# Two key blocks per values matmul, a query with x stationary, and output products in two column tiles

## The chip, the cores and the metric

The kernel runs on one core of a Trainium2 chip. A core has a matrix engine (PE, with its weight loads shown apart as PEld), a vector engine (DVE), a scalar engine (ACT), a general engine (POOL), a sync engine (SP) that here issues nearly all loads, and sixteen DMA engines that move data between memory and the core's on-chip memory (SBUF). Matmul results go to PSUM, a second on-chip memory [...]. The metric is the time of one execution on the device in microseconds; the number compared is the median of several runs.

## The reference

A decode step for eight tokens mixes an attention branch and an MLP branch with a gate.

```python
def _A_ref(x, k_cache, v_cache, wq, wo):      # B=8, Sq=1, D=448, Hq=16, Hkv=8, Sk=4096, Dh=256
    W = min(4096, max(256, Sk // 4))          # 1024: only the last 1024 keys are used
    q = (x @ wq).reshape(B, Sq, Hq, Dh).transpose(0, 2, 1, 3)
    k = jnp.repeat(k_cache[:, :, Sk - W:, :], 2, axis=1)
    v = jnp.repeat(v_cache[:, :, Sk - W:, :], 2, axis=1)
    p = softmax(einsum("bhqd,bhkd->bhqk", q, k) * Dh ** -0.5)
    o = einsum("bhqk,bhkd->bhqd", p, v)
    return o.transpose(0, 2, 1, 3).reshape(B, Sq, Hq * Dh) @ wo
def _B_ref(x, w1, b1, w2, b2):                # F=1792
    y = layernorm(x)
    return gelu(y @ w1 + b1) @ w2 + b2
g = sigmoid((x * gate_w).sum(-1))
return g * _A_ref(x, ...) + (1 - g) * _B_ref(x, ...)
```

Everything is bf16 in memory. Keys and values of the window are 8 x 8 x 1024 x 256 elements each, 67 MB together; the four weight matrices add 10.6 MB.

## The kernel before

**Units.** The work on the cache is cut into 16 units (NQ), one for each token and each half of the eight key heads. A unit is four key heads (QUAD) with two query heads each, so eight query rows (RQ). Its keys are one load of 2 MB, its values another; in SBUF 32 partitions belong to one key head, and each partition holds 32 keys (NCK) of 256 elements.

**Loads.** `plan` is the list of all large loads in order: keys of unit 0, w1, the two parts of wq, w2, then keys of unit u and values of unit u-3 in turn, the last three values, and wo in six pieces. They pass through a ring of nine slots of 2 MB; `done()` marks slots as used up and lets `pump()` hand the next loads to SP's queue, where each waits for its slot. Instruction order on each engine is the order in which the Python code emits it (the schedule is manual).

**Per unit.** `transpose_keys` turns the keys with 64 PE transposes (L323) into PSUM and copies them out with ACT and DVE (L326, L328). `scores` multiplies them with the query rows, 16 matmuls of 512 columns in four column tiles of the PE array: each tile has its own 32 partitions of the result `S_ps`, and tiles run side by side. `top`, `expo`, `turn` and `bring` are the softmax of the unit before, placed between the transposes; `bring` leaves the turned weights in ET, 32 key blocks of eight columns, and `rsel`, which holds one over the row sum at the query rows' own places and zero elsewhere (`sel`). `values` (L416) streams the value rows of the 32 key blocks: 32 matmuls with an eight-column stationary block of ET and 256 columns of values, in turn into four column tiles of the PSUM tile PO, each accumulating eight blocks. DVE copies PO to `os_` (L430). `finish` multiplies `os_` with `rsel`, which picks for each query row the right row of `os_` and sums the four tiles, and writes the result into oT.

**Head.** Before the loop over units come `norm_and_gate`, the transposes of unit 0, `mlp_hidden` (the product with w1 and the activation), `query` (L333: 128 matmuls with a block of wq stationary and the eight tokens moving, result `qt` with the head dimension on partitions, eight scaled copies into qw), `scores` of unit 0 and `mlp_out` (L493: for each of 14 blocks of w2, and once for b2, four matmuls, one for each quarter of the 448 output columns, in four column tiles given by `quads`).

**Tail.** After the last unit's values and `finish`, `spread_rows` brings oT into a layout with all 128 partitions in use (oP), in two halves. `project` (L556) multiplies oP with wo: 32 steps j, each four matmuls of 112 columns in the four column tiles of `quads`, accumulating in A_ps. The order of issue is spread_rows of the first half, values and finish of the last unit, spread_rows of the second half, then the four calls of project; each waits for its piece of wo, of which the last comes in three parts. One DVE operation (L577) combines A_ps with the gate and the MLP output `mixb` into `res`, and four stores (L587), two issued by SP and two by ACT, write the four column quarters.

Of the kernel before, what the change touches and what calls it, by code (L numbers as in the profile page):

```python
# [8 lines left out]
ACT = mybir.ActivationFunctionType  # L9
ALU = mybir.AluOpType  # L10
AXIS = mybir.AxisListType
BF16 = mybir.dt.bfloat16
F32 = mybir.dt.float32
# [4 lines left out]
def kernel(  # L18
# [15 lines left out]
    nc = tc.nc  # L34
    P = nc.NUM_PARTITIONS

    NB, Sq, D = A_x.shape
    _, Hkv, Sk, Dh = A_k_cache.shape
    HD = A_wq.shape[1]
    Hq = HD // Dh  # L40
    rep = Hq // Hkv
    W = min(4096, max(256, Sk // 4))
# [3 lines left out]
    NJ = Dh // P  # L46
    NC = W // P
    NR = 3
# [2 lines left out]
    NF = F // P  # L51
    FH = F // 2
    HH = HD // 2
    QUAD = 4
    RQ = QUAD * rep
    NQ = NB * Hkv // QUAD
    SK = P // QUAD
    NCK = W // SK
# [10 lines left out]
    qscale = float(Dh) ** -0.5  # L69
# [118 lines left out]

    S_ps = ps_s.tile([P, W], F32)
    nc.vector.memset(S_ps[:], 0.0)  # L190
    PO = ps_po.tile([P, Dh], F32)
    nc.vector.memset(PO[:], 0.0)

    NX = NR + 2
    DQ = D // QUAD

    def quads(ps):
        return [
            (ps[32 * i : 32 * i + NB, :], slice(i * DQ, (i + 1) * DQ))
            for i in range(QUAD)  # L200
        ]

    xz = consts.tile([NB, 2, P], BF16)
# [3 lines left out]
    xT = consts.tile([P, NX, NB], BF16)  # L207
    yT = consts.tile([P, NX, NB], BF16)
    sel = consts.tile([P, RQ], F32)
    qw = consts.tile([P, NJ, NB, Hq // RQ, QUAD, RQ], BF16)  # L210
    oT = consts.tile([P, Hq, NJ, NB], BF16)
    gg = consts.tile([NB, 2], F32)
    spread = consts.tile([NB, QUAD, 32], F32)
    gg_s = consts.tile([P, 2], F32)
    ones_r = consts.tile([1, NB], BF16)
    mixb = consts.tile([P, DQ], F32)
    res = consts.tile([P, DQ], BF16)
    nc.vector.memset(spread[:], 0.0)
    nc.vector.memset(ones_r[:], 1.0)

# [8 lines left out]
    for h in range(2):  # L229
        nc.vector.tensor_copy(xz[:, h, h::2], x_sb[:, DM:D])  # L230
    transposed(xT, x_sb, xz)
    nc.vector.reduce_sum(
        sel[:], ident[:].rearrange("p (a s) -> p s a", a=QUAD)[:, 0:RQ, :], axis=AXIS.X
    )
    perm = consts.tile([P, P], BF16)
    nc.vector.tensor_copy(
# [5 lines left out]
    for a in range(QUAD):  # L242
# [3 lines left out]
            axis=AXIS.X,  # L246
# [6 lines left out]
    def norm_and_gate():  # L253
        stats = consts.tile([NB, nc.vector.BN_STATS_DIM], F32)
        nc.vector.bn_stats(stats[:], x_sb[:])
        mv = consts.tile([NB, nc.vector.BN_AGGR_DIM], F32)
        nc.vector.bn_aggr(mv[:], stats[:])
        eps_t = consts.tile([NB, 1], F32)
        nc.vector.memset(eps_t[:], 1e-5)
        rstd = consts.tile([NB, 1], F32)  # L260
        nc.scalar.activation(rstd[:], mv[:, 1:2], ACT.Sqrt, bias=eps_t[:], scale=1.0)
        nc.vector.reciprocal(rstd[:], rstd[:])
        y_sb = consts.tile([NB, D], BF16)
        nc.vector.tensor_scalar(
            y_sb[:],
            x_sb[:],
            scalar1=mv[:, 0:1],
            scalar2=rstd[:],
            op0=ALU.subtract,
            op1=ALU.mult,  # L270
        )
        for h in range(2):
            nc.vector.tensor_copy(yz[:, h, h::2], y_sb[:, DM:D])
        transposed(yT, y_sb, yz)
        prod = consts.tile([NB, D], F32)
        gl = consts.tile([NB, 1], F32)
        nc.vector.scalar_tensor_tensor(
            prod[:],
            in0=x_sb[:],
            scalar=1.0,  # L280
            in1=gw_b[:],
            op0=ALU.mult,
            op1=ALU.mult,
            accum_out=gl[:],
        )
        gth = consts.tile([NB, 1], F32)
        nc.scalar.activation(gth[:], gl[:], ACT.Tanh, scale=0.5)
        nc.vector.tensor_scalar(
            gg[:, 0:1], gth[:], 0.5, 0.5, op0=ALU.mult, op1=ALU.add
        )  # L290
        nc.vector.tensor_scalar(
            gg[:, 1:2], gth[:], -0.5, 0.5, op0=ALU.mult, op1=ALU.add
        )
        nc.vector.tensor_copy(
            spread[:, :, 0:NB],
            ident[0:NB, 0:NB]
            .rearrange("p (o b) -> p o b", o=1)
            .to_broadcast([NB, QUAD, NB]),
        )
        gp = ps_misc.tile([P, 2], F32, tag="misc", name="gp")  # L300
        nc.tensor.matmul(
            gp[:],
            lhsT=spread[:].rearrange("p i b -> p (i b)"),
            rhs=gg[:],
            start=True,
            stop=True,
        )
        nc.vector.tensor_copy(gg_s[:], gp[:])
# [22 lines left out]
        done()  # L331

    def query():  # L333
        qt = ps_misc.tile([P, Hq * NJ, NB], F32, tag="misc", name="qt")
        for r in range(NR + 1):
            w, o = slot("wq", r // 2), (r % 2) * HD
            for k in range(Hq * NJ):
                col = (k // NJ) * Dh + (k % NJ) * P
                half, c = divmod(col, HH) if r == NR else (0, col)
                nc.tensor.matmul(  # L340
                    qt[:, k, :],
                    lhsT=w[:, o + c : o + c + P],
                    rhs=xT[:, r + half, :],
                    start=(r == 0 and k == 0),
                    stop=(r == NR),
                    skip_group_check=True,
                )
        done(2)
        qv = qt[:].rearrange("p (g a i j) b -> p a j b g i", g=Hq // RQ, a=QUAD, i=rep)
        for a in range(QUAD):  # L350
            for j in range(NJ):
                nc.vector.tensor_scalar_mul(  # L352
                    qw[:, j, :, :, a, a * rep : (a + 1) * rep], qv[:, a, j], qscale
                )

    def scores(u):
# [37 lines left out]
    def bring(u):  # L394
        EB, selr = soft.pop(u)
        sm = ps_sm.tile([P, NCK + 1, RQ], F32, tag="sm", name="sm")
        nc.tensor.matmul(  # L397
            sm[:, 0:NCK, :], lhsT=perm[:], rhs=EB[:, :, 0:RQ], start=True, stop=True
        )
        nc.tensor.matmul(sm[:, NCK, :], lhsT=ones_f[:], rhs=selr[:], start=True, stop=True)  # L400
        ET = opool.tile([P, NCK, RQ], BF16, tag="ET", name="ET")
        nc.vector.tensor_copy(ET[:], sm[:, 0:NCK, :])  # L402
        rb = epool.tile([P, RQ], F32, tag="rb", name="rb")
        nc.vector.reciprocal(rb[:], sm[:, NCK, :])
        rsel = opool.tile([P, RQ], F32, tag="rsel", name="rsel")
        nc.vector.tensor_tensor(rsel[:], rb[:], sel[:], op=ALU.mult)
        soft[u] = (ET, rsel)

    def steps(u):
# [6 lines left out]
    def values(u):  # L416
        ET, rsel = soft.pop(u)
        vn = slot("v", u)
        for c in range(NCK):
            t = c % QUAD  # L420
            nc.tensor.matmul(  # L421
                PO[32 * t : 32 * t + RQ, :],
                lhsT=ET[:, c, 0:RQ],
                rhs=vn[:, c * Dh : (c + 1) * Dh],
                start=(c < QUAD),
                stop=(c >= NCK - QUAD),
            )
        done()
        os_ = epool.tile([P, Dh], F32, tag="os", name="os_")
        nc.vector.tensor_copy(os_[:], PO[:])  # L430
        soft[u] = (os_, rsel)

    def finish(u):
# [57 lines left out]
        return hs  # L491

    def mlp_out(hs):  # L493
        bb = ps_misc.tile([P, DQ], F32, tag="misc", name="bb")
        nc.vector.memset(bb[:], 0.0)
        for c in range(NF):
            w = slot("w2")
            for dst, cols in quads(bb):
                nc.tensor.matmul(
                    dst,  # L500
                    lhsT=hs[:, c, :],
                    rhs=w[:, c * D + cols.start : c * D + cols.stop],
                    start=(c == 0),
                    stop=False,
                )
        for dst, cols in quads(bb):
            nc.tensor.matmul(
                dst, lhsT=ones_r[:], rhs=b2_r[:, cols], start=False, stop=True
            )
        done()  # L510
        nc.vector.tensor_scalar_mul(mixb[:], bb[:], gg_s[:, 1:2])
# [20 lines left out]
    finish(u - 2)  # L532
    bring(u)
    values(u - 1)
    A_ps = ps_misc.tile([P, DQ], F32, tag="misc", name="A_ps")
    nc.vector.memset(A_ps[:], 0.0)
    finish(u - 1)
    oP = consts.tile([P, NJ8, NHQ, NB], BF16)
# [17 lines left out]
    def project(q):  # L556
        w = slot("wo", q - q % 2)
        for j in range(NJ8):
            o = ((q % 2) * NJ8 + j) * D
            for dst, cols in quads(A_ps):  # L560
                nc.tensor.matmul(  # L561
                    dst,
                    lhsT=oP[:, j, q, :],
                    rhs=w[:, o + cols.start : o + cols.stop],
                    start=(q == 0 and j == 0),
                    stop=(q == NHQ - 1 and j == NJ8 - 1),
                )
# [14 lines left out]
        op0=ALU.mult,  # L582
        op1=ALU.add,
    )
    for i, (src, cols) in enumerate(quads(res)):
        eng = nc.sync if i % 2 == 0 else nc.scalar
        eng.dma_start(out_f[:, cols], src)  # L587

# [29 lines left out]
```

## Time and profile before

| | us |
|---|---|
| median of 9 runs | 195.43 |
| lowest and highest | 195.28, 195.67 |
| the profiled execution | 195.28 |
| its span, first to last instruction | 193.5 |
| PE busy | 148.6 (77%) |
| PE weight loads busy | 110.7 (57%) |
| DVE busy | 112.4 (58%) |
| ACT busy | 82.9 (43%) |
| data moved | 78.02 MB, mean 403 GB/s |

The profile is of one execution. Its span is cut into 40 equal slices; in the rows of digits each digit is the busy share of a slice in tenths, and PEclk is the clock that the matrix engine was granted, in tenths of full speed. The queue rows give packets, megabytes and the time of the packets as a share of sixteen DMA engines over the span. Lines of the timeline give start, duration, engine, source line, operation, result and operands, count, and in brackets how long the engine had been idle before it and what ended the wait. Windows give the same measures for a stretch of time. The chain follows the work that ended last back to what released it.

### The profile page before, as it was taken

How to read it: one execution, taken by the hardware profiler on the slowest of the kernel's cores; microseconds unless marked ns; L12 is line 12 of the kernel's file. 1: busy time of each engine (PE TensorE's matmuls, PEld its weight loads, DVE VectorE, ACT ScalarE, POOL GpSimd, SP SyncE). 2: the span in 40 equal slices, each digit the busy share in tenths (PEclk: the TensorE clock that was granted, in tenths of full speed). 3: DMA queues.
4: the chain of work that ended last, by engine and by line, in shares of the span. 5: the costliest groups of instructions: out<-in, count | busy, mean ns of one | idle time of the engine just before them, and what ended most of it. 6: DMA issues, size and time to landing. Idle time of an engine off the chain costs nothing.

```text
span 193.5 us, 5200 instructions
## 1 busy us (share of the span) xinstructions
PE 148.6 (77%) x2334; PEld 110.7 (57%) x2334; DVE 112.4 (58%) x259; ACT 82.9 (43%) x101; POOL 0.8 (0%) x7
## 2 busy tenths in 40 slices
PE   1399968989999898987768787877878787946652
PEld 0399927675665767574637373737474646534441
DVE  7531342787866869684747575666666666653100
ACT  2352003675754828372708182827272727320000
POOL 1000000000000000000000000000000000000000
PEclk9997566999999999999999999999999999995555
DMA  4999999999999999999999999999999999999960
GB/s 176 428 423 415 432 424 428 417 430 423 430 423 430 420 423 423 427 425 423 423 430 423 430 417 425 423 427 427 427 430 423 427 417 430 420 423 422 407 248 7
DMA packets 6744, 78.02 MB, mean 403 GB/s; under 512 B 945, under 2 KB 1346, under 8 KB 1986
## 3 DMA queue, kind: packets, MB, share of 16 engines
q1 hardware_dynamic: 6512, 77.67, 95.3%
q8 instruction: 18, 0.29, 0.6%
q10 hardware_dynamic: 210, 0.02, 0.2%
q14 instruction: 4, 0.03, 0.0%
HBM read 77.68 MB, written 0.01 MB: 401 GB/s over the span
## 4 chain that ended last, share of the span: by engine, by line
DMA 86%; PE 7%; ACT 4%; ACTq 1%; issue 0%; DVE 0%; SPq 0%
DMA slot<-in_A_k_cache_dram 51%; DMA slot<-in_A_v_cache_dram 20%; DMA slot<-in_A_wo_dram 10%; DMA b_sb<-in_B_b_dram 4%; PE ktp L323 4%; ACT kt L326 3%; PE S_ps L361 2%; ACT E L381 1%; PE PO L421 1%; ACTq L174 0%; PE A_ps L561 0%; DVE res L577 0%; PE sm L400 0%; ACTq L181 0%; ACTq L178 0%
## 5 line engine op out<-in xcount | busy, mean ns | idle before, releaser
L326 ACT COPY kt<-ktp 128x1024 bf16<-128x1024 bf16 x64 | 63.2, 1017 | 74.4 <-PE ktp L323 74.4
L323 PE MATMUL ktp<-ident,slot 128*128 128x128 bf16 x1024 | 71.1, 226 | 22.3 <-ACT kt L326 10.8
L323 PEld LDWEIGHTS <-slot 128*128 128x128 bf16 x1024 | 65.0, 103 | 29.4 <-issue 16.1
L328 DVE COPY kt<-ktp 128x1024 bf16<-128x1024 bf16 x64 | 41.3, 684 | 16.4 <-PE ktp L323 16.4
L373 DVE TENSOR_REDUCE nmx<-S_ps 128x1 f32<-128x1024 f32 x16 | 19.6, 1225 | 22.6 <-PE S_ps L361 22.6
L361 PE MATMUL S_ps<-kt,qw 128*8 128x512 bf16 x256 | 32.3, 627 | 0.3 <-DVE qw L352 0.3
L389 DVE STREAM_TRANSPOSE EB<-E 128x1024 bf16<-128x1024 bf16 x16 | 19.9, 1245 | 7.2 <-ACT E L381 6.9
L421 PE MATMUL PO<-slot,ET 128*8 128x256 bf16 x512 | 18.4, 290 | 3.4 <-DMA slot<-in_A_v_cache_dram 3.4
L381 ACT ACTIVATE E<-S_ps,nmx 128x1024 bf16<-128x1024 f32 x16 | 17.9, 1120 | 3.3 <-DVE nmx L374 3.3
L421 PEld LDWEIGHTS <-ET 128*8 128x8 bf16 x512 | 11.9, 90 | 6.7 <-issue 3.5
L361 PEld LDWEIGHTS <-qw 128*8 128x8 bf16 x256 | 7.3, 95 | 12.0 <-issue 10.4
L402 DVE CAST ET<-sm 128x256 bf16<-128x256 f32 x16 | 6.6, 414 | 0.5 <-PE sm L400 0.5
L561 PE MATMUL A_ps<-slot,oP 128*8 128x112 bf16 x128 | 4.1, 291 | 2.4 <-DMA slot<-in_A_wo_dram 2.3
L400 PE MATMUL sm<-selr,ones_f 128*128 128x8 f32 x32 | 5.2, 233 | 0.0
L441 DVE CAST oT<-sm 128x16 bf16<-128x16 f32 x16 | 3.5, 219 | 2.8 <-PE sm L438 2.8
L400 PEld LDWEIGHTS sm<-selr,ones_f 128*128 128x128 f32 x32 | 4.8, 188 | 0.4 <-issue 0.4
L561 PEld LDWEIGHTS <-oP 128*8 128x8 bf16 x128 | 2.9, 114 | 3.4 <-issue 3.4
L397 PE MATMUL sm<-EB,perm 128*128 128x256 bf16 x16 | 4.4, 272 | 0.3 <-DVE oT L441 0.3
L340 PE MATMUL qt<-xT,slot 128*128 128x8 bf16 x128 | 3.6, 168 | 0.4 <-DVE z L471 0.4
L340 PEld LDWEIGHTS <-slot 128*128 128x128 bf16 x128 | 3.6, 104 | 0.4 <-issue 0.3
L577 DVE SCALAR_TENSOR_TENSOR res<-A_ps,gg_s,mixb 128x112 bf16<-128x112 f32 x1 | 0.3, 333 | 5.9 <-PE A_ps L561 5.9
L471 DVE TENSOR_TENSOR z<-hT,b_sb 128x112 f32<-128x112 f32 x1 | 0.3, 275 | 5.5 <-PE hT L461 5.5
(122 smaller groups left out, 75.5 us busy)
## 6 DMA issues: line engine op xcount, KB each, us to landing
slot<-in_A_v_cache_dram SPq DMA_DIRECT2D x16, 2048.0 KB, 38.8
slot<-in_A_k_cache_dram SPq DMA_DIRECT2D x15, 2048.0 KB, 36.0
slot<-in_A_wo_dram SPq DMA_DIRECT2D x3, 896.0 KB, 32.1
slot<-in_A_k_cache_dram SPq DMA_DIRECT2D x2, 1024.0 KB, 7.5
slot<-in_A_wq_dram SPq DMA_DIRECT2D x1, 2048.0 KB
slot<-in_B_w_dram SPq DMA_DIRECT2D x1, 1568.0 KB
slot<-in_B_w_dram SPq DMA_DIRECT2D x1, 1344.0 KB, 10.2
slot<-in_A_wq_dram SPq DMA_DIRECT2D x1, 1024.0 KB
```

The lines of the kernel that those rows point to most:

```text
L323: nc.tensor.transpose(ktp[:, c, :], kn[:, o : o + P], ident[:])
L326: nc.scalar.copy(dst, ktp[:])
L328: nc.vector.tensor_copy(dst, ktp[:])
L340: nc.tensor.matmul(qt[:, k, :], lhsT=w[:, o + c : o + c + P], rhs=xT[:, r + half, :], start=(r == 0 and k == 0), stop=(r == NR), skip_grou ...
L361: nc.tensor.matmul(S_ps[32 * a : 32 * a + RQ, hf * CH * SK : (hf + 1) * CH * SK], lhsT=qw[:, j, b, half, a, :], rhs=KT[hf][:, j, :, a::QUA ...
L373: nc.vector.reduce_max(nmx[:], S_ps[:], axis=AXIS.X, negate=True)
L381: nc.scalar.activation(E[:], S_ps[:], ACT.Exp, bias=nmx[:], scale=1.0, accum_out=rowsum[:])
L389: nc.vector.transpose(EB[:].rearrange("p c r -> p (c r)"), E[:])
L400: nc.tensor.matmul(sm[:, NCK, :], lhsT=ones_f[:], rhs=selr[:], start=True, stop=True)
L402: nc.vector.tensor_copy(ET[:], sm[:, 0:NCK, :])
L421: nc.tensor.matmul(PO[32 * t : 32 * t + RQ, :], lhsT=ET[:, c, 0:RQ], rhs=vn[:, c * Dh : (c + 1) * Dh], start=(c < QUAD), stop=(c >= NCK - ...
L561: nc.tensor.matmul(dst, lhsT=oP[:, j, q, :], rhs=w[:, o + cols.start : o + cols.stop], start=(q == 0 and j == 0), stop=(q == NHQ - 1 and j ...
```

## The change

There are four edits, and some constants and masks for them.

Values: the stationary operand is two key blocks of ET side by side (16 columns), the moving operand the two blocks' values side by side (512 columns). The product holds four parts, of which only the two with equal block are wanted: rows 0 to 7 of a tile with the first 256 columns, rows 8 to 15 with the second. [...] In place of the copy, one DVE operation multiplies the first half by a mask (`own`, column 0) and a second adds the second half times the other mask (column 1); `rsel` is built with `sel2`, which has a one at both places of a query row.

Query: x is stationary (eight columns) and wq moves in 512 columns, into four column tiles of S_ps, 32 matmuls; ACT copies the result with the scale to bf16, eight transposes of 128 x 128 bring the head dimension to partitions, and eight DVE copies write qw.

MLP output and projection: `halves` takes the place of `quads`: two column tiles, at partitions 0 and 64, of 224 columns each. The tiles bb, A_ps, mixb and res are twice as wide, and there are two stores of the output, one issued by SP and one by ACT.

```diff
-    PO = ps_po.tile([P, Dh], F32)
+    PO = ps_po.tile([P, PAIR, Dh], F32)          # PAIR = 2
...
-    def quads(ps):
+    def halves(ps):
         return [
-            (ps[32 * i : 32 * i + NB, :], slice(i * DQ, (i + 1) * DQ))
-            for i in range(QUAD)
+            (ps[64 * i : 64 * i + NB, :], slice(i * DO, (i + 1) * DO))   # DO = 224
+            for i in range(OT)                                           # OT = 2
         ]
...
+    halfs = ident[:].rearrange("p (a s) -> p s a", a=QUAD)
+    for i in range(PAIR):
+        nc.vector.reduce_sum(
+            own[:, i : i + 1], halfs[:, i * RQ : (i + 1) * RQ, :], axis=AXIS.XY
+        )
+    nc.vector.reduce_sum(
+        sel2[:],
+        ident[:]
+        .rearrange("p (a h s) -> p s a h", a=QUAD, s=RQ)[:, :, :, 0:PAIR],
+        axis=AXIS.XY,
+    )
...
     def query():
-        qt = ps_misc.tile([P, Hq * NJ, NB], F32, tag="misc", name="qt")
         for r in range(NR + 1):
             w, o = slot("wq", r // 2), (r % 2) * HD
-            for k in range(Hq * NJ):
-                col = (k // NJ) * Dh + (k % NJ) * P
-                half, c = divmod(col, HH) if r == NR else (0, col)
-                nc.tensor.matmul(
-                    qt[:, k, :],
-                    lhsT=w[:, o + c : o + c + P],
-                    rhs=xT[:, r + half, :],
...
+            for n in range(W // QN):                                     # QN = 512
+                for t in range(QUAD):
+                    col = t * W + n * QN
+                    half, c = divmod(col, HH) if r == NR else (0, col)
+                    nc.tensor.matmul(
+                        S_ps[32 * t : 32 * t + NB, n * QN : (n + 1) * QN],
+                        lhsT=xT[:, r + half, :],
+                        rhs=w[:, o + c : o + c + QN],
...
         done(2)
-        qv = qt[:].rearrange("p (g a i j) b -> p a j b g i", g=Hq // RQ, a=QUAD, i=rep)
+        qs = consts.tile([P, W], BF16)
+        nc.scalar.activation(qs[:], S_ps[:], ACT.Copy, scale=qscale)
+        qt = ps_kt.tile([P, NC, P], BF16, tag="ktp", name="qt")
+        for m in range(NC):
+            nc.tensor.transpose(qt[:, m, :], qs[:, m * P : (m + 1) * P], ident[:])
+        qv = qt[:].rearrange(
+            "p (c i j) (g d s) -> p d c j s g i", c=2, i=rep, j=NJ, g=Hq // RQ, d=2
+        )
         for a in range(QUAD):
             for j in range(NJ):
-                nc.vector.tensor_scalar_mul(
-                    qw[:, j, :, :, a, a * rep : (a + 1) * rep], qv[:, a, j], qscale
+                nc.vector.tensor_copy(
+                    qw[:, j, :, :, a, a * rep : (a + 1) * rep],
+                    qv[:, a // 2, a % 2, j, 0:NB],
                 )
...
-        nc.vector.tensor_tensor(rsel[:], rb[:], sel[:], op=ALU.mult)
+        nc.vector.tensor_tensor(rsel[:], rb[:], sel2[:], op=ALU.mult)
...
     def values(u):
-        for c in range(NCK):
+        NG = NCK // PAIR
+        for c in range(NG):
             t = c % QUAD
             nc.tensor.matmul(
-                PO[32 * t : 32 * t + RQ, :],
-                lhsT=ET[:, c, 0:RQ],
-                rhs=vn[:, c * Dh : (c + 1) * Dh],
+                PO[32 * t : 32 * t + PAIR * RQ],
+                lhsT=ET[:, PAIR * c : PAIR * (c + 1), :],
+                rhs=vn[:, PAIR * c * Dh : PAIR * (c + 1) * Dh],
...
-        nc.vector.tensor_copy(os_[:], PO[:])
+        nc.vector.tensor_scalar_mul(os_[:], PO[:, 0, :], own[:, 0:1])
+        nc.vector.scalar_tensor_tensor(
+            os_[:], in0=PO[:, 1, :], scalar=own[:, 1:2], in1=os_[:],
+            op0=ALU.mult, op1=ALU.add,
+        )
...
-            for dst, cols in quads(bb):
+            for dst, cols in halves(bb):        # and the same for b2, A_ps and res
```

## The prediction

> **What bounds the kernel now.** I read the slices first, then the chain that ended last, then the queues.
>
> ```profile
> PEclk9997566999999999999999999999999999995555
> DMA  4999999999999999999999999999999999999960
> DMA 86%; PE 7%; ACT 4%; ACTq 1%; issue 0%; DVE 0%; SPq 0%
> q1 hardware_dynamic: 6512, 77.67, 95.3%
> q8 instruction: 18, 0.29, 0.6%
> ```
>
> The DMA engines are full from the second slice to the next-to-last, and the chain is 86% transfers. So time is won in two ways only: the last transfer lands sooner, or less work follows it. PE's clock is halved in the last four slices, which matters for that work. The q8 row is the third thing to see: 18 packets that carry instructions, 0.6% of 16 engines' 193.5 us, so 18.6 us of engine time or 1.03 us each, 16 KB each.
>
> Next the end of the load stream in half-microsecond windows (the last two columns are the DMA share and GB/s):
>
> ```profile
> 184.50:185.00 0.50, 0.50 1.05 416
> 185.50:186.00 0.50, 0.50 0.60 233
> 187.50:188.00 0.50, 0.50 0.51 190
> 188.50:189.00 0.50, 0.50 0.07 25
> 189.00:189.50 0.50, 0.50 0.05 18
> ```
>
> The stream does not stop at once. From 185.3 about nine engines of sixteen still work (0.55 to 0.61), and from 188.2 only one (1/16 is 0.06). The trace's landing marks, one per engine and transfer, say the same: of the last wo piece the first mark is at 185.23, the fifteenth at 188.75, the sixteenth at 189.84. One engine ends 1.09 us after all others, and the kernel waits for it.
>
> Why is it late? I set the start of each q8 packet against the PE instructions started by then (a matmul and its weight load are two): the 9th at 91.0 us against 2254, the 17th at 180.9 against 4348, the 18th at 188.0 against 4588. That is one packet per 256 instructions. In the marks, at 80.25 the last engine is 0.04 us behind the fifteenth, but after the 9th packet one mark lies 1.08 us behind the other fifteen (100.95 against 99.87), after the 10th two do, after the 16th eight do; after the 17th one is alone again (185.35 against 184.25). I read this as eight engines taking the packets in turn, each losing about 1.08 us per packet; the one that gets the 1st, 9th and 17th decides the end.
>
> **The change part by part.** *PE's instruction count.* Values: 32 matmuls become 16 in each of 16 units, -256. Query: 128 become 32 and 8 transposes, -88. MLP output: 60 become 30, -30. Projection: 128 become 64, -64. Together -438 of 2334, leaving 1896, or 3792 PE instructions with the weight loads: 14 packets (3584) and not a 15th (3840). No engine then gets a third. In before, after 14 packets and until the 17th, the marks lay 3.54 us from first to last (151.82 to 155.36, 171.43 to 174.97); the first mark of the last piece, 185.23, belongs to an engine that takes no packets. New end: 185.23 + 3.52 to 3.54 = 188.75, **1.09 us sooner**. The other wo pieces move alike: 182.1, 184.25, 186.45, 187.6, 188.2.
>
> Here a rule speaks against the change. The Trainium skill, "Runtime: NRT & Kernel Launch", section Instruction fetch mechanics, says that fetches come in 16 KiB blocks of 256 instructions (the trace agrees) and that crossing a block costs "one DMA tail-bump, mostly hidden". By it this term is 0. It is hidden for PE, but the row has 1.03 us of one engine per packet, and here the slowest engine sets the end. I take the row. A bound on the other side: VectorE's own code grows by about 19 instructions, and a further fetch on q14 (8 KB, some 0.3 us each) may fall on the last engine: 0 to +0.3, I take 0.
>
> *The head.* Three reduces (L232's row has 0.20 for one) and a larger PO memset (+0.27) delay VectorE by 0.9. Query: 32 matmuls of 512 columns cost 3.4 to 5.1 at half clock (16 of the scores' took 2.55 at 25.08) against 3.55, then an activation over 1024 elements (L381: 1.12) and 8 transposes (0.6 to 0.9), then eight copies as before (0.9). mlp_out takes up to 1.7 more. In all 3 to 7 us later. What hides it:
>
> ```profile
> 51.45 0.54 SPq L109 DMA_DIRECT2D slot<-in_A_v_cache_dram  x1
> 52.44 0.54 SPq L109 DMA_DIRECT2D slot<-in_A_k_cache_dram  x1
> 60.94 0.54 SPq L109 DMA_DIRECT2D slot<-in_A_k_cache_dram  x1
> slot<-in_A_v_cache_dram SPq DMA_DIRECT2D x16, 2048.0 KB, 38.8
> ```
>
> The load issued at 51.45 lands at 80.25, 28.8 us later, when its own transfer is some 4.9: about 24 us of loads stand queued at the thinnest place, so slots given back 7 us late starve nothing. Beyond 24 us each further one would be paid in full. I price the head at 0.
>
> *The loop.* Values stream 16 x 512 columns instead of 32 x 256, in four tiles as before: no change. VectorE gets two masked operations for one copy. The copy is 0.425 (L430, 256 elements). L511 and L577, the same two forms on 112 elements, took 0.333; one element more costs 0.95 ns (L402's 256 took 414 ns, L552's 128 took 292), 144 more 0.14, so 0.47 each and 0.03 between: 0.97, **+0.55 per unit**. While it catches up, PE gives K slots back every 8.1 to 8.5 us (the lines above); with 0.55 that stays under the 9.8 us in which a unit's K and V land. Price 0, until a unit costs more than 9.8.
>
> *The tail.* Here nothing covers:
>
> ```profile
> 181.84 0.42 DVE L430 COPY os__3037<-PO 128x256 f32<-128x256 f32 x1 [2.36 <-PE PO L421]
> 185.39 0.92 PE L561 MATMUL A_ps<-slot,oP 128*8 128x112 bf16 x32 [0.62 <-DMA slot<-in_A_wo_dram]
> 187.57 0.92 PE L561 MATMUL A_ps<-slot,oP 128*8 128x112 bf16 x32 [1.27 <-DMA slot<-in_A_wo_dram]
> 189.88 0.36 PE L561 MATMUL A_ps<-slot,oP 128*8 128x112 bf16 x8 [0.22 <-DMA slot<-in_A_wo_dram]
> 190.29 0.33 DVE L577 SCALAR_TENSOR_TENSOR res<-A_ps,gg_s,mixb 128x112 bf16<-128x112 f32 x1 [5.91 <-PE A_ps L561]
> 190.65 0.70 SPq L587 DMA_DIRECT2D out_dram<-res  x2
> ```
>
> The last V lands at 179.88 in both kernels (the 17th packet comes after it). Behind the PO copy queue finish, spread_rows and project, so project starts at 183.78 + 0.55 = 184.33. One step j streams two tiles of 224 columns instead of four of 112. At the halved clock 256 columns took 0.213 (values at 179.92: 8 rounds in 1.88 less a 0.2 drain), so 224 take 0.187 and all 32 rounds **5.97 instead of 2.99**. In before projection waited for each wo piece; now the pieces come sooner and PE is behind them. Cold all the way it ends at 184.33 + 5.97 + 0.18 drain = 190.48, where before ended at 190.25. Warm soon enough, it ends 0.35 after the last landing: 188.79 + 0.35 = 189.14.
>
> Will it warm? "TensorE: Matmul & The Clock Gate" (Trainium skill, Part 1) says that the clock goes up after a busy window of about 3.4 us, free-running. The trace's clock steps lie on such a grid (17.16, 27.40, 30.82, 34.23, 174.18). In the window 23.99 to 27.40, 2.3 us of streaming (scores) were enough; in 174.18 to 177.59, 1.9 us (values) were not. By the row the clock rises at the first grid point after 184.33 + 2.2 = 186.5, somewhere up to 189.9 as the grid falls; its middle is 188.2. Half of what is then left remains: 188.2 + (190.30 - 188.2)/2 = 189.25, drain 0.17. By the rule's full window the middle is 189.5 and streaming ends at 189.9. I take the row, as it is this kernel's own streaming.
>
> Then res: 0.333 + 112 x 0.95 ns = 0.44 (+0.11). Output: each queue issues one transfer instead of two; the four landed at 191.87, 192.04, 192.25 and 192.47, and the first two remain: **-0.43**.
>
> *Sum.* Res ends at 189.42 + 0.04 + 0.44 = 189.90 against 190.62: -0.72; with the output -1.15. The profiled execution took 195.28 (span 193.5, 1.78 around it), so 194.13; the median of the runs, 195.43, is 0.15 above it, so **194.3**. By the clock rule's window it would be -0.50, 194.9; by the fetch rule (no sooner landing) about 195.1.
>
> **Rivals.** *Projection stays cold* (two tiles may not count as busy): res ends at 190.96, +0.34, with the output -0.09: 195.3. For: the clock never rose in the old tail. Against: there PE streamed under 2 us per window, here without a break. *The packets don't decide the end* (another order of engines, or a late q14 fetch): landing 189.84 as now, q3 streams behind it, res ends 0.1 to 0.6 later: 195.1 to 195.6. Against: marks and packets match one by one. *Two tiles don't overlap* (slower): each round costs two streams. Cold that would be 64 x 0.187 = 12.0 and end at 196.5; with the clock up from about 187.5 it ends near 192.0, so res at 192.6, +2.0, less 0.43: 197.0. It decides as soon as a cold round takes over 0.20. For: no pair of tiles 64 apart is in the trace. Against: four tiles do overlap (32 matmuls of 112 columns in 0.92).
>
> **How the numbers follow.** Likeliest case 0.70 (its own range, over the grid, 193.9 to 195.1), cold 0.17, packets don't decide 0.07, no overlap 0.06. The range takes in all but the last: 193.8 to 195.6. A difference of 0.2%, 0.39 us, is about what can be told here: faster 0.71 (nearly all of the first case, little of the third), same 0.22, slower 0.07.
>
> **What would show it.** q8 with 14 packets; no window with one engine alone; last wo landing near 188.75; project starting near 184.33 and streaming without gaps; clock back to full between 186.5 and 190; the res operation at 0.44; two output transfers. The prediction is wrong if the head empties the queue (a gap in the DMA slices), if a unit passes 9.8 us, or if the number of PE instructions is not 3792.

## The result, and the profile after

The changed kernel takes **194.53 us** in the median (194.04 to 194.82, ten runs), the kernel before 195.52 (195.28 to 195.79, 31 runs). The ratio is **0.9947, with a 95% interval of 0.9939 to 0.9955**: 0.99 us faster, where 1.15 was forecast. The execution that was profiled took 194.64 with a span of 192.9, so it shows only 0.6 of the gain in span. That difference is one of the things to explain.

The page of the changed kernel, first its span, the clock and DMA slices, the queues and the shares of the chain:

```profile
span 192.9 us, 4344 instructions
PEclk9999697999999999999999999999999999975559
DMA  5999999999999999999999999999999999999960
q1 hardware_dynamic: 6496, 77.67, 95.5%
q8 instruction: 15, 0.25, 0.5%
DMA 60%; PE 24%; ACT 7%; DVE 5%; issue 1%; ACTq 0%; SPq 0%; DVEq 0%
```

The loads fill the DMA slices as before. Instruction packets on q8 fell from 18 to 15, and the clock is back at full in the last slice. In before the chain that ended last came in through the last wo load (start, length, what):

```profile
170.13 19.71 DMA slot<-in_A_wo_dram
```

Now it comes in through the last values load, which landed at 179.89, and from there it runs over values, masked operations, finish and spread to projection without another load. Of the lines from there on, two:

```profile
179.93 1.91 PE PO L446 x13
184.68 4.75 PE A_ps L594 x63
```

So projection, not its data, is what ends last. The end of the load stream in half-microsecond windows (length, clock, DMA share, GB/s):

```profile
185.50:186.00 0.50, 0.50 0.62 244
187.50:188.00 0.50, 0.50 0.33 112
188.50:189.00 0.50, 1.00 0.00 0
189.00:189.50 0.50, 1.00 0.00 0
```

In before, the windows from 188.5 still showed one engine (0.07 and 0.05). Here they are empty. The landing marks of the last wo piece say it exactly: fourteenth 188.26, fifteenth 188.31, sixteenth 188.72; before they were 188.75 for the fifteenth and 189.84 for the sixteenth. The timeline of the tail (start, length, engine, operation):

```profile
181.86 0.48 DVE L455 TENSOR_SCALAR os__2685<-PO,own 128x256 f32<-128x256 f32 x1 [1.71 <-PE PO L446]
182.38 0.48 DVE L456 SCALAR_TENSOR_TENSOR os__2685<-PO,own,os__2685 128x256 f32<-128x256 f32 x1
184.50 4.92 PE L594 MATMUL A_ps<-slot,oP 128*8 128x224 bf16 x63
189.46 0.45 DVE L610 SCALAR_TENSOR_TENSOR res<-A_ps,gg_s,mixb 128x224 bf16<-128x224 f32 x1 [4.41 <-PE A_ps L594]
189.93 0.37 SPq L620 DMA_DIRECT2D out_dram<-res  x1
```

The two masked operations stand where one copy stood. Projection runs in one piece without waiting for wo, and `res` ends at 189.91 instead of 190.62. The last store lands at 191.35 instead of 192.47, 1.12 sooner. Yet the span is only 0.6 shorter: half a microsecond was lost behind the last store. It is in SP's instructions of the kernel's close, where SP waits for one pair of semaphores (the counters by which a transfer tells that it has landed) after the other (shortest, median and longest in ns, then first and last start), of the kernel before:

```profile
L613 SPq EVENT_SEMAPHORE  x7: 17/28/28, 192.3 to 193.4; - x7
```

and of the changed one:

```profile
L646 SPq EVENT_SEMAPHORE  x7: 17/28/1013, 190.4 to 192.8; - x7
```

In before, SP's instruction behind the last store's landing came 0.02 us after it (192.47, 192.49). In the changed kernel the first closing wait lasts 1013 ns, from 190.36 to 191.37. It ends 0.02 after the landing, but the next instruction comes only at 191.81, 0.46 after the landing.

| us | before | predicted | after |
|---|---|---|---|
| last wo landing | 189.84 | 188.75 | 188.72 |
| projection starts | 183.78 | 184.33 | 184.45 |
| clock up in the tail | not | 188.2 | 188.01 |
| `res` operation | 0.33 | 0.44 | 0.45 |
| `res` ends | 190.62 | 189.90 | 189.91 |
| last store lands | 192.47 | not given | 191.35 |
| SP goes on | 192.49 | not given | 191.81 |

### The profile page after: what moved, and what is told of

Read it like the earlier page. It is cut to its first block, busy times and chain, and to the rows that moved or that the text cites. A ratio compares the mean times of both kernels' runs of the same rounds, so it can differ in the third digit from the quotient of the medians.

```text
span 192.9 us, 4344 instructions
## 1 busy us (share of the span) xinstructions
PE 150.5 (78%) x1896; PEld 103.7 (54%) x1896; DVE 121.9 (63%) x278; ACT 83.8 (43%) x102; POOL 0.9 (0%) x7
## 4 chain that ended last, share of the span: by engine, by line
DMA 60%; PE 24%; ACT 7%; DVE 5%; issue 1%; ACTq 0%; SPq 0%; DVEq 0%
DMA slot<-in_A_k_cache_dram 40%; DMA slot<-in_A_v_cache_dram 20%; PE ktp L339 7%; PE S_ps L385 4%; ACT kt L342 4%; PE A_ps L594 2%; ACT E L405 2%; PE PO L446 2%; PE S_ps L356 2%; PE hT L494 2%; PE bb L532 1%; PE hT L484 1%; PE sm L471 1%; DVE nmx L397 1%; ACT qs L366 1%
## 5 line engine op out<-in xcount | busy, mean ns | idle before, releaser
L339 PE MATMUL ktp<-ident,slot 128*128 128x128 bf16 x1024 | 69.7, 223 | 20.2 <-ACT kt L342 11.6
L339 PEld LDWEIGHTS <-slot 128*128 128x128 bf16 x1024 | 63.6, 101 | 27.4 <-issue 17.2
L446 PE MATMUL PO<-slot,ET 128*16 128x512 bf16 x256 | 18.3, 410 | 1.4 <-DMA slot<-in_A_v_cache_dram 1.3
L446 PEld LDWEIGHTS <-ET 128*16 128x16 bf16 x256 | 5.4, 91 | 7.2 <-issue 2.6
L594 PE MATMUL A_ps<-slot,oP 128*8 128x224 bf16 x64 | 5.0, 338 | 0.0
L594 PEld LDWEIGHTS <-oP 128*8 128x8 bf16 x64 | 4.7, 113 | 0.0
L532 PE MATMUL bb<-slot,hs 128*8 128x224 bf16 x28 | 2.8, 388 | 1.9 <-DVE bb L528 1.9
L532 PEld LDWEIGHTS <-hs 128*8 128x8 bf16 x28 | 1.6, 122 | 3.5 <-DVE bb L528 2.8
L356 PE MATMUL S_ps<-slot,xT 128*8 128x512 bf16 x32 | 3.3, 589 | 0.0
```

Source lines behind the costliest of these rows:

```text
L339: nc.tensor.transpose(ktp[:, c, :], kn[:, o : o + P], ident[:])
L356: nc.tensor.matmul(S_ps[32 * t : 32 * t + NB, n * QN : (n + 1) * QN], lhsT=xT[:, r + half, :], rhs=w[:, o + c : o + c + QN], start=(r == 0 ...
L446: nc.tensor.matmul(PO[32 * t : 32 * t + PAIR * RQ], lhsT=ET[:, PAIR * c : PAIR * (c + 1), :], rhs=vn[:, PAIR * c * Dh : PAIR * (c + 1) * D ...
L594: nc.tensor.matmul(dst, lhsT=oP[:, j, q, :], rhs=w[:, o + cols.start : o + cols.stop], start=(q == 0 and j == 0), stop=(q == NHQ - 1 and j ...
```

## The experiments

The theory: a third instruction packet on one DMA engine made the last wo landing late, and 438 matmuls fewer (876 PE instructions with their weight loads) take it away. Its rivals: the gain is the shorter output (two stores for four) or the wider projection, and packets have nothing to do with it. The ratios below are each against runs of the kernel before on the same chip.

**Values alone** (e1). Only the two-block values matmul and its masks; `quads`, four stores and the old query stay.

```diff
-        for c in range(NCK):                       # 32 matmuls of 256 columns
+        for c in range(NCK // PAIR):               # 16 matmuls of 512 columns
...
-        nc.vector.tensor_copy(os_[:], PO[:])
+        nc.vector.tensor_scalar_mul(os_[:], PO[:, 0, :], own[:, 0:1])
+        nc.vector.scalar_tensor_tensor(os_[:], in0=PO[:, 1, :], scalar=own[:, 1:2], in1=os_[:], op0=ALU.mult, op1=ALU.add)
```

> The kernel before with the values edit alone (two key blocks per matmul, masks). 2078 matmuls, 4156 PE instructions with their weight loads: 16 instruction packets, no engine gets a third. Theory of the last engine: the last wo piece lands at 188.7 instead of 189.84, the projection keeps its four tiles and starts at 184.3, res ends 0.36 + 0.04 + 0.33 after the landing at 189.5, so about 1.1 us less than before: 194.4. Rival (the gain of the whole change comes from the wider tiles and the two stores): landing as before, 195.4.

It took 194.56 in the median, ratio 0.9940 (0.9928 to 0.9953): the whole gain of the change, with four stores and four column tiles. There are 16 packets, and the last two marks lie at 189.12 and 189.16, none alone. The landing came 0.68 sooner than in before, not the 1.1 that were expected: already the first mark of the piece was 0.30 later (185.53 against 185.23). `res` ended at 189.94, 0.68 sooner as well. The clock never came up in its tail, and with four tiles that cost nothing. So neither stores nor projection are needed for the gain.

**Column halves alone** (e2). MLP output and projection in two tiles and two stores; values and query as before.

```diff
-    def quads(ps):                                 # four tiles of 112 columns
+    def halves(ps):                                # two tiles of 224 columns, two stores
```

> The kernel before with the two column tiles alone (MLP output, projection, gate spread, two stores). 2240 matmuls, 4480 PE instructions: 17 packets, the 17th near 184. Theory of the last engine: the packet still falls on the engine that decides, the last wo piece lands near 189.84, projection streams behind it; the two stores save 0.4 of landing, the wider res costs 0.11, the wider projection 0 to 0.5: 195.2 to 195.6, and up to 196.0 if the program's end waits 0.44 longer for two stores, as it did in the changed kernel. Rival (the gain is in the tiles and stores): 194.5.

195.24, ratio 0.9984 (0.9970 to 0.9997). It keeps 17 packets, and one mark stays alone: 188.58, then 189.76 for the sixteenth. `res` ended at 190.66, as in before. The last store landed at 192.10, 0.37 sooner, and SP's closing wait took 1028 ns, with the next instruction at 192.57, 0.47 after the landing. In the trace the saved stores come back almost whole as that wait; the runs keep at most 0.6 us of it.

**Query alone** (e3). Stationary x, eight transposes; nothing else.

```diff
-            for k in range(Hq * NJ):               # 128 matmuls, wq stationary
+            for n in range(W // QN):               # 32 matmuls, x stationary, 512 columns
...
+        for m in range(NC):
+            nc.tensor.transpose(qt[:, m, :], qs[:, m * P : (m + 1) * P], ident[:])
```

> The kernel before with the query edit alone. 2246 matmuls, 4492 PE instructions: 17 packets, the 17th (instruction 4352) shortly before the projection, near 184. Theory of the last engine: this packet still delays the engine that ends last; landing near 189.84 and 195.4, no change within 0.2%, although one packet in 18 is gone. Rival (each packet costs its share of all sixteen engines, 1.03/16 = 0.065 us): also about 195.4, so this run alone does not tell these two apart; together with the values edit it does (two packets less: 195.3 by the share, 194.4 by the last engine).

195.75, ratio 1.0010 (0.9999 to 1.0021): no change. The 17th packet was taken at 187.7, later than expected, and the last mark stands alone again, at 190.45 against 189.14 for the fifteenth. The head's cost is hidden, and 88 matmuls fewer leave the third packet in place.

**The changed kernel, padded** (e4). 25 tiny matmuls, whose product nothing reads, in each of the 15 units of the loop bring the PE instructions back.

```diff
+    dm = ps_misc.tile([P, NB], F32, tag="misc", name="dm")
...
+        for _ in range(25):
+            nc.tensor.matmul(dm[0:NB, :], lhsT=ident[:, 0:NB], rhs=ident[:, 0:NB], start=True, stop=True)
```

> The changed kernel with 25 matmuls of 8 columns that nothing reads at the end of each of 15 units, 375 in all: 2271 matmuls, 4542 PE instructions, 17 packets, the third packet of the first engine near 181. Theory of the last engine: the wo pieces land 1.1 us later than in the changed kernel (last one 189.84), the last mark alone by 1.1 us; with the projection's two tiles streaming behind it res ends near 190.7 instead of 189.9: 0.8 us more than the changed kernel, about 195.3. Rival (packets don't decide the end; the extra matmuls are hidden in PE's idle time of the loop): as the changed kernel, 194.5.

196.81, ratio 1.0057 (1.0037 to 1.0077), well beyond the 195.3 expected. The last landing did go back, from 188.72 to 189.72, with 18 packets taken in the whole run, though its last mark stands alone by 0.56 only. But projection began only at 186.04, 1.6 late, and `res` ended at 192.59: the padding itself delayed the tail. It decides nothing about the time. e7 and e8 avoid this.

**Values and query, without the halves** (e7), as in the diffs of e1 and e3 together, and **the same, padded early** (e8): 29 unread matmuls in units 1 to 12 only, so that the last three units run undisturbed.

```diff
+        for _ in range(29 if u <= 12 else 0):
+            nc.tensor.matmul(dm[0:NB, :], lhsT=ident[:, 0:NB], rhs=ident[:, 0:NB], start=True, stop=True)
```

> The changed kernel without the two column tiles: values and query edits, projection and MLP output in four tiles of 112, four stores. 1990 matmuls, 3980 PE instructions, 15 packets. If the last landing decides: lands at 188.7, the projection keeps pace with the wo pieces even at half clock, res ends at 189.5, stores as before, 1.1 us less than before: 194.4. Against the changed kernel this trades a projection that may run 0 to 1.3 us behind for 0.4 us of store landing, so its runs should spread less. Rival (two tiles were worth something): 194.9 or more.

> The values-and-query kernel (projection in four tiles, four stores) with 29 matmuls of 8 columns that nothing reads at the end of units 1 to 12, 348 in all, and none in the last units, so that the tail starts as before: 2338 matmuls, 4676 PE instructions, 18 packets, the 17th near 180. Theory of the last engine: the last wo piece lands 1.1 us later again (189.8, its last mark alone by about 1.1) and the time returns to that of the kernel before, 195.4 to 195.7. Rival (fewer instructions help in another way, or by 0.065 us for each packet's share of sixteen engines): 194.3 to 194.5.

e7 took 194.31, ratio 0.9936 (0.9923 to 0.9949), e8 195.48, 0.9990 (0.9979 to 1.0002). The intervals are far apart: matmuls whose product no one reads cost 1.17 us by the medians, 1.06 by the ratios (the two ran on different chips). The queue row and the last windows of e7:

```profile
q8 instruction: 15, 0.25, 0.5%
...
187.50:188.00 0.50, 0.50 0.36 129
188.50:189.00 0.50, 0.50 0.00 0
```

and of e8:

```profile
q8 instruction: 18, 0.29, 0.6%
...
187.50:188.00 0.50, 0.50 0.51 190
188.50:189.00 0.50, 0.50 0.10 36
189.00:189.50 0.50, 0.50 0.07 25
```

The one engine is back from 188.5 on (0.07 is about 1/16). The mark of the last V already stands alone by 0.92 (180.35, then 181.27), after the 17th packet at 178.1, and that of wo by 0.93 (189.22, then 190.15). Projection waited for each piece, and `res` ended at 190.93 instead of 189.48. The last landing came 1.45 later than in e7 (190.15 against 188.70), of which 0.93 are the lone mark's. The rival that the padding held the whole load stream up does not fit: the first mark of the last wo piece was not later than in e7 (185.32 against 185.46). This is the landing theory with about its size, in a kernel in which nothing else of the change was touched.

**Four stores again** (e5). The changed kernel with `res` written by two stores on each queue.

```diff
-        eng = nc.sync if i % 2 == 0 else nc.scalar
-        eng.dma_start(out_f[:, cols], src)
+        for h in range(2):
+            eng = nc.sync if h == 0 else nc.scalar
+            eng.dma_start(out_f[:, cols.start + h * HO : cols.start + (h + 1) * HO], src[:, h * HO : (h + 1) * HO])
```

> The changed kernel with four stores of 112 columns, two on each queue, from the same two row groups of res. In the changed kernel the last store lands 1.12 us sooner than before, but the span is only 0.6 shorter: after SP's first closing wait, satisfied at 191.37, the next instruction comes 0.44 later, where before it came 0.06 later. Theory of the slow closing wait (SP reaches the wait before the store lands and is slow to leave it when the semaphore is the second of its two): with four stores the last to land are again those of the first semaphores, so landing is 0.4 later and the wait 0.4 shorter: 194.5, as the changed kernel. Plain theory (a store more costs its issue): 194.9.

195.00, ratio 0.9954 (0.9941 to 0.9968), not to be told from the changed kernel's 0.9947. From the end of `res` to the last store's landing it took 1.84 us (190.77 to 192.61), as before had (1.85), against 1.44 in the changed kernel; so one store fewer per queue is worth 0.41. But SP went on 0.02 after the landing. What the stores cost here, the quick wait gives back.

Its `res` ended 0.86 later than in the changed kernel, though projection started at 184.56. The cause is the clock: it rose at 189.66 and not at 188.01.

```profile
184.62 5.67 PE L594 MATMUL A_ps<-slot,oP 128*8 128x224 bf16 x63
```

The same 63 matmuls took 4.92 in the changed kernel. The steps of the clock lie 3.41 us apart, and where they fall differs from run to run, so a projection that is wide and at half clock makes the time itself uncertain by some 0.7 us. In e5 the runs fit this: the six below 194.5 have a mean granted clock of 0.938 to 0.956, the eleven others 0.909 to 0.927. The spread of the changed kernel's runs, 194.04 to 194.82, is of that size too, but there the clock does not sort them (0.929 to 0.952 in the five quickest, 0.935 to 0.956 in the others), so for them this cause is not shown.

**The first load in four parts** (e6). This shifts which semaphore each later transfer uses, and so the place of the output stores among the closing waits.

```diff
-    add_kv("k", A_k_cache, 0, parts=2)
+    add_kv("k", A_k_cache, 0, parts=4)
```

> The changed kernel with the first key load cut into four parts instead of two, which does nothing to the loads' total but moves the two stores to other semaphores, each the first in its closing wait. Theory of the slow closing wait: 0.4 us off, 194.1, with SP's wait left within 0.1 of the landing. Rival (the 0.44 belongs to the program's end whatever the semaphore): 194.5.

A miss: 195.48, ratio 0.9991 (0.9975 to 1.0006), where 194.1 was expected. SP did go on at once, 0.01 after the last landing (192.96, 192.97). But the last wo landing came at 189.56, 0.84 later than in the changed kernel. The first mark of that piece was only 0.25 later (185.43 against 185.18) and the fourteenth 1.18 (189.44 against 188.26): the engines ended 4.13 us apart instead of 3.54. They had drifted apart long before, with as many packets (15). Soon after the first packet (in the load that landed at 27.35 here, at 25.94 in the changed kernel) one mark already lay 1.46 behind the fifteenth, against 0.76; after the ninth packet the gap from first to last was 4.08 against 2.93 (loads landing at 116.99 and 115.61). The clock also rose late, at 190.2. Why finer first loads pull the engines apart stays open.

**Two wo pieces in two parts each** (e10). The same shift of the semaphores, made near the end of the loads.

```diff
-    WO_PARTS = [[(0, NJ8)]] * (NHQ - 1) + [[(0, 4), (4, 6), (6, 8)]]
+    WO_PARTS = [[(0, 4), (4, 8)]] * 2 + [[(0, NJ8)], [(0, 4), (4, 6), (6, 8)]]
```

> The changed kernel with the first two wo pieces cut in two, which leaves the last pieces as they are and moves the two stores to semaphores that come first in SP's closing waits. Theory of the slow closing wait: SP's wait ends within 0.1 us of the last store's landing instead of 0.46, so 0.4 less than the changed kernel: 194.1, with the same spread. Rival: 194.5, no change.

194.16, ratio 0.9927 (0.9900 to 0.9954). The closing wait is short again:

```profile
L646 SPq EVENT_SEMAPHORE  x7: 17/28/28, 191.1 to 192.2; - x7
```

The last store landed at 191.27 and SP went on at 191.28; the span is 192.3 instead of 192.9. By the trace the wait is worth 0.44. The medians differ by 0.37, but their intervals overlap, so the runs alone do not prove it.

**PE kept streaming** (e9). 26 rounds of four matmuls of 512 columns, whose products nothing reads, in PE's waiting times of the tail (after the values and spreads of the last three units), to keep the clock up.

```diff
+    def stream(rounds):
+        for _ in range(rounds):
+            for a in range(QUAD):
+                nc.tensor.matmul(S_ps[32 * a : 32 * a + RQ, 0:QN], lhsT=qw[:, 0, 0, 0, a, :], rhs=KT[1][:, 0, 0:QUAD, :], start=True, stop=True)
...
     values(u)
+    stream(5)
```

> The changed kernel with streaming matmuls that nothing reads (4 tiles of 512 columns, 26 rounds in all) in PE's waits of the tail, between 170.8 and 183, so that PE's clock need not fall before the projection. Theory of the cold projection: the projection starts at 183.4 to 184.4 with the clock at full and takes 3 us of streaming instead of 4.97, keeps up with the wo pieces, ends 0.36 after the last landing (189.1); res ends at 189.6 wherever the clock's grid falls: 194.0 to 194.3, with little spread. Rival (the clock or the two tiles do not hold the projection up): as the changed kernel, 194.5, spread over 0.8.

**194.03, ratio 0.9911 (0.9894 to 0.9928): the lowest median of all.** The interval lies clear of the changed kernel's (0.9939 to 0.9955). Windows one clock step long, with PE's busy time (instructions), clock, DMA share and GB/s; of the changed kernel:

```profile
177.77:181.18 3.41, 2.63 (x36) 0.50 0.98 404
181.18:184.60 3.42, 1.91 (x31) 0.50 1.00 409
184.60:188.01 3.41, 3.41 (x48) 0.50 0.54 208
188.01:191.42 3.41, 1.41 (x29) 1.00 0.01 3
```

and of e9:

```profile
177.77:181.18 3.41, 3.14 (x72) 1.00 0.97 402
181.18:184.60 3.42, 2.86 (x62) 1.00 1.01 403
```

With the clock up, projection again waits for wo, as in before, and ends right behind it:

```profile
188.43 0.36 PE L607 MATMUL A_ps<-slot,oP 128*8 128x224 bf16 x4 [0.21 <-DMA slot<-in_A_wo_dram]
```

`res` ended at 189.28 instead of 189.91. Of these 0.63 us, 0.34 came with the landing (188.38 instead of 188.72; the eleventh to fifteenth marks lie where they were, within 0.05, and why the last came sooner is open; with the same streaming e11 landed at 188.92). The other 0.29 are what the clock is worth by the trace: in e9 projection ended 0.40 behind the last landing, in the changed kernel 0.70. The slow closing wait was still there (1020 ns; landing 190.72, SP on at 191.17).

**Both together** (e11: e9 and e10) and **with streaming inside projection too** (e12: six more rounds after the second call of `project`).

```diff
     for q in range(NHQ):
         project(q)
+        if q == 1:
+            stream(6)
```

> Both of these in the changed kernel. If both theories hold: last landing 188.7, res ends at 189.6, stores land at 191.05, no slow wait: span 192.1, 193.8 to 193.9, less than any kernel so far. If only one holds: 194.1 to 194.3.

> The changed kernel with the streaming in the tail, the first two wo pieces cut in two, and six more streaming rounds (24 matmuls that nothing reads) in PE's 1.6 us wait between the second and the third projection call, where the clock fell in the profile of the run before (at 186.9) and the projection ended at 189.65. Theory of the cold projection: the clock stays at full to the end, the projection ends 0.36 after the last landing, res at 189.6, no slow closing wait, 193.8. Rival (the streaming itself holds the wo pieces or the third call up): 194.1 or more.

194.14, ratio 0.9912 (0.9894 to 0.9930), and 194.10, 0.9916 (0.9899 to 0.9934): neither beats e9, though 193.8 or a little more was expected, and none of the three can be told from the others by its interval. Beside e10 alone (194.16) the streaming of e11 brought 0.02 us in the median, with overlapping intervals. SP went on 0.01 to 0.02 after the landing in both. In e11's profile the clock fell at 186.9, where PE had waited 1.64 us for wo, and `res` ended at 190.14. In e12 the clock stayed up but the last wo landing was 188.92 against 188.38 in e9. What the short wait gave was lost there, in e11 to the clock as well; whether the cut of the wo pieces causes the later landing (188.90 in e10, 188.92 in e11) was not tested.

## Why the prediction was right, and where not

**Packets and the last landing.** Right in kind and size: 188.75 predicted, 188.72 measured. e1 shows that the values edit alone brings the time, and e7 against e8 that more packets take it away (+1.17). Over all fourteen kernels the last mark of the last wo piece stood alone by 0.56 to 1.31 us in the five with 17 or 18 packets, and by 0.43 at most in the nine with 15 or 16. That the landing was met to 0.03 is luck: in the nine kernels it fell between 188.38 (e9) and 189.56 (e6). Here the rule and the row parted. The Trainium skill, "Runtime: NRT & Kernel Launch", section Instruction fetch mechanics, as the prediction read it, would have priced it at 0, and the row of 1.03 us per packet was the right one to take. Hidden for PE did not mean hidden for the DMA engine that the fetch occupies.

The count was wrong by one: 15 packets, not 14. The last was taken at 187.6, with 3,734 of 3,792 PE instructions started, where the prediction's count put a 15th at 3,840. So a packet can be taken ahead of that count, as the 18th in before had been already, by less (at 4588, where 18 times 256 is 4608). It was without consequence: in the wo piece that landed at 186.45, before this packet, the last mark already lay 0.39 behind the fifteenth, as it does in the last piece (0.41). And 15 packets on eight engines in turn give none of them a third either.

**Head and loop.** Right at 0. Query took 3.32 us of matmuls, 1.02 of activation, 0.62 of transposes and 0.87 of copies; the transposes of unit 1 began at 34.03 instead of 30.98, 3.1 late (3 to 7 predicted), and the DMA slices stayed at 9. The masked operations took 0.96 for 0.42. e3 agrees for the head, e1 for the loop.

**Projection.** The working held to 0.12 us at its start and 0.19 at the clock step; `res` ended at 189.91 for 189.90. The last two are luck: the step was forecast as the middle of a range from 186.5 to 189.9, and in e5 it came at 189.66, in e10 at 187.43. What the working left unsaid is that the wider projection is a loss beside the narrow one: with four tiles (e7) and the same landing (188.70), `res` ended at 189.48 with the clock down throughout. The runs as a whole don't tell the two kernels apart.

Of the rules on the clock, the changed kernel's own window cannot choose, since 184.60 to 188.01 was busy throughout. e2 and e4 can. In e2 the clock rose at 188.71, after a window with a wait of 0.62 us for wo in it; in e4 it did not rise at 188.42, but one step later, at 191.83:

```profile
185.30:188.71 3.41, 2.79 (x32) 0.50 0.41 161
185.01:188.42 3.41, 3.10 (x46) 0.50 0.50 198
```

So a window without a gap, as the prediction read "TensorE: Matmul & The Clock Gate", Part 1, was not needed. But the prediction's own row, a rise after 2.2 us of streaming, fails too: in e4 projection had streamed for 2.4 us of that window (from 186.04). The row had been read from a window with 2.3 us of scores in which PE was busy for 3.13 us in all (23.99 to 27.40). What counts in a window stays open.

**Output stores: the step that failed.** The prediction counted -0.43 for two output transfers fewer. The way from `res` to the landing gained 0.41, as said. But it was taken for granted, without a term, that the program's close follows the landing as it did in before. It did not: 0.44 of it came back behind SP's first closing wait. This is why the profiled execution gained 0.64 and not 1.15. The median gained 0.99, because the profiled execution of before was the fastest of its 31 (195.28, 0.24 below the median) and that of the changed kernel lay 0.11 above its median. Five runs of the changed kernel lie between 194.04 and 194.37 and five between 194.70 and 194.82, the profiled one (194.64) near these; what the quicker five did otherwise no trace tells.

## What to carry to other kernels

In a kernel whose DMA engines are full, count instructions as bytes: here every 256 PE instructions cost one of sixteen engines mostly 1.0 to 1.1 us, and the engine with one packet too many stood 0.6 to 1.3 us behind the others at the end. Look at the landing marks of the last load one by one: here a single late mark was work for the instruction count, not for bandwidth. Fewer and wider matmuls in an uncovered tail at half clock can cost more than they save (`res` at 189.91 against 189.48). Streaming unread work ahead of it kept the clock up; the median fell by 0.5 us (194.53 to 194.03), of which the trace gives 0.29 to the clock, and beside e10 the same streaming brought nothing that could be told.

## What the hardware showed that was not expected

Each of SP's closing waits names two semaphores. In four kernels (the changed one, e2, e4, e9) the last store to land counted on the second semaphore of the first wait, and SP's next instruction came 0.45 to 0.47 us after the landing. In the other ten, before included, it counted on the first semaphore of the second wait, and the next instruction came 0.01 to 0.02 after it. e6 and e10 moved the stores to other semaphores and the delay went. That the first wait is slow whatever it waits for does not fit: in e10 the store of its first semaphore landed at 191.06, and the wait was over at 191.11. Why the second place is slower no run shows.

Instruction packets put some of the engines behind the others: between the first and the last mark of the last wo piece lay 3.2 to 4.1 us in the kernels with 15 or 16 packets. That they fall on eight of the sixteen engines in turn is the reading that fits the 17th packet best (it makes one mark stand alone again, as the 9th does), but it is not shown: after the 16th packet nine marks of before lie in the late group (174.07 to 174.97), not eight. Which engines these are stays open, as does the wider gap of e6.
